# A fused attention and token mixer: the paired last tokens get their attention rows by copies and one add, and the written-out order is new behind the first up projection

## The chip, the core and the metric

The kernel runs on one core of one Trainium2 chip. The metric is the device time of one execution in microseconds. The core has a matrix engine (TensorE, PE in the profile, with its weight loads as PEld), a vector engine (VectorE, DVE), a scalar engine (ScalarE, ACT), a general engine (GpSimd, POOL) and an engine that only issues transfers here (SyncE, SP). Each engine executes its own instructions in the order in which the program gives them; engines wait for one another on semaphores. Matmul results go to eight banks of 512 floats per partition, and VectorE or ScalarE must move them out (evict them) before a bank can be filled again.

## What is computed

Eight batches, eight heads, 576 tokens, head dimension 64. Attention is causal in blocks of 64 tokens; its output is laid out as x of 576 tokens by 512 channels per batch and goes through a mixer: one two-layer network over the tokens, one over the channels, each with a residual.

```python
scores = scale * np.matmul(q, k.transpose(0, 1, 3, 2))
scores = np.where(block_i >= block_j, scores, -1e9)      # blocks of 64
attn = softmax(scores);  x = attn @ v                    # then (B, 576, 512)
h  = np.maximum(x.T @ w_tok1, 0.0) @ w_tok2              # 576 -> 256 -> 576
u  = x + h.T
h2 = np.maximum(u @ w_ch1, 0.0) @ w_ch2                  # 512 -> 1536 -> 512
out = u + h2
```

## The kernel before

**An order written out by hand.** Every step of the kernel is registered with `Plan.add` as an operation with a number, the engines that may run it, its dependencies and a function that issues its instructions. `ORDER` (from L100) is one long string: each word is an operation's number and a letter for its engine (T TensorE, A ScalarE, D VectorE, P GpSimd, S SyncE), followed, for an operation that opens a bank, by the letter of the bank (a to d are the tiles `mm`, e to h the tiles `late`). `Plan.placed` walks through the words and issues the operations, so the string sets the order on every engine, the engine of each eviction and the bank of each product. The planner's costs and priorities in `P.add` play no part in it any more.

**Tiles and stages.** A batch's 576 tokens are four chunks of 128 and a last one of 64. For each batch, `load_qk` loads K and Q for four heads at a time (GpSimd issues the transfer, L418) and VectorE transposes them in 32x32 blocks (L442). `load_v` loads V in pieces J = 0 to 4, one for each chunk (L468, pieces J = 0 to 3 of 128 KB and J = 4 of 64 KB). `score_set` (L566) makes the scores of two or four heads, ScalarE takes their exponential into `e_sb` (L772), `tail` copies the last 64 columns aside (L594) and clears them (L599). `head_out` multiplies the exponentials with V for the four chunks of a head (L616; VectorE's reciprocal L636 and multiply L642 write x into `x_sb`), and `ends_out` does the last 64 tokens (L669, L691, L697).

**The last tokens.** `ends_out` writes chunk 4 of `x_sb` with the heads interleaved: even heads lie on partitions 0 to 63, odd heads on partitions 64 to 127, in 256 columns. A 64-row chunk would leave half of every later product empty, so `token_mix` pairs the last 64 tokens of two batches, b-1 and b for odd b, into one tile `um_sb[:, pair]` of 128 rows by 512 channels. The four pairs together are treated as a ninth batch, the mixed one, at the end.

**The mixer.** `token_up` makes the token hidden layer `aT`. `token_mix` multiplies it with w_tok2 into a bank for each chunk (L902), and VectorE adds x to it on its way into `u_sb` (L917). For a pair it does eight matmuls of the w_tok2 columns 512 to 576 (L933) into the two halves of one bank, and then four matmuls with the identity (L942), which add the attention rows to the bank and put even and odd heads in their columns. An eviction by ScalarE (L400) or VectorE (L402) casts the bank into `um_sb`. u is then transposed, by TensorE for batch 1 and its pair (L989) and by transfers for later ones (L979). The channel layers are `channel_up` for batch 0, `channel_up_half` for batches 1 to 3 and the mixed one and `channel_up_fast` for pairs of later batches; `channel_down_fast` (L1364) makes the last product and folds partial sums and the residual into `o_sb` (L1410). These use fewer products by sums and differences of weights and inputs that VectorE makes first (L1061, L1075, L1316, L1346).

**Around the change.** The order before and the order after hold the same words up to 306P, a tail copy on GpSimd at 31.9 us; from there they differ. Numbers that the prediction names: 264 to 268 are V pieces J = 0 to 4 of batch 1; 427 and 430 are the loads of K and Q for the second four heads of batch 2, and 428 one of VectorE's transposes of that K; 167 to 169 are the first three pieces of w_ch2 (wc2, 512 KB each, L511); 445 is a score set of batch 2 and 624 one of batch 3; 492 is VectorE's multiply that ends a head of batch 2 and, in the new order, frees a bank that 624 takes; 1546 and 1547 are output transfers of the mixed batch, 1558 and 1559 a product and a fold of the last batch, 1590 the last output. TensorE is then in the channel up products of batch 0. `EVAC` marks evictions that VectorE or ScalarE may do, `TAILS` small copies that VectorE or GpSimd may do:

```python
EVAC = ("DVE", "ACT")
TAILS = ("DVE", "POOL")
```

## Time and profile before

| what | value |
| --- | --- |
| time, median of 3 runs (lowest to highest) | 284.84 us (284.7 to 284.98) |
| span of the profiled execution | 283.1 us |
| granted TensorE clock | 0.999 |
| TensorE busy | 276.5 us, 98% of the span |
| VectorE busy, instructions | 239.1 us, 84%, 515 |
| ScalarE busy, instructions | 179.3 us, 63%, 331 |
| GpSimd busy, instructions | 72.4 us, 26%, 126 |
| HBM read, written | 35.85 MB, 9.44 MB |

The span is what the profiler saw from the first to the last instruction; the time of a run holds some 1.8 us around it. A row of a timeline gives the start in us, the length in us, the engine, the line in the kernel, the operation, output and inputs, and in square brackets how long the engine stood idle before it and what ended that. PE rows in which many matmuls are put together give the length of the whole group. "issue" means a wait that the profile shows no cause for. A row for a load ends with the kilobytes of one transfer and the median time in us from issue to landing. In a table of windows each engine has its busy time and the number of its instructions.

### The profile page before, as it was taken

What the parts mean: (1) busy time and instruction counts of PE and PEld (TensorE: products, weight loads), DVE (VectorE), ACT (ScalarE), POOL (GpSimd) and SP (SyncE); (2) the same over time, 40 slices, a digit from 0 to 9 for tenths busy, and PEclk for the clock granted to TensorE, in tenths of its full rate; (3) what the DMA queues carried; (4) which work ended last, traced back from release to release, by engine and by line L of the source; (5) the groups of instructions that cost most, each with busy time, mean ns of one, the idle gap of its engine ahead of it and who ended that gap; (6) DMA issues with size and microseconds to landing.
All of it is one profiled execution on the core that took longest, in us unless ns stands there. A gap on an engine that the chain in (4) does not pass through costs nothing.

```text
span 283.1 us, 9609 instructions
## 1 busy us (share of the span) xinstructions
PE 276.5 (98%) x4110; PEld 204.7 (72%) x4110; DVE 239.1 (84%) x515; ACT 179.3 (63%) x331; POOL 72.4 (26%) x126
## 2 busy tenths in 40 slices
PE   8999999999999999999999999999999999999995
PEld 3566656588776788986877658756789876568884
DVE  4578669999889898999998979959897897579984
ACT  3798788953998856897779866274533744652200
POOL 8885760511631351063232221000000000000000
PEclk9999999999999999999999999999999999999999
DMA  7999999955989792999698595100044502100157
GB/s 174 161 181 198 198 195 200 140 89 113 109 97 135 81 153 55 165 194 166 72 117 144 43 195 67 59 21 19 0 78 91 206 0 76 74 2 2 74 151 223
DMA packets 64891, 31.97 MB, mean 113 GB/s; under 512 B 53200, under 2 KB 55888, under 8 KB 64848
## 3 DMA queue, kind: packets, MB, share of 16 engines
q0 software_dynamic: 44896, 17.49, 53.8%
q1 hardware_dynamic: 19520, 13.21, 19.7%
q8 instruction: 32, 0.52, 0.8%
q10 hardware_dynamic: 432, 0.66, 0.7%
q14 instruction: 11, 0.09, 0.1%
HBM read 35.85 MB, written 9.44 MB: 160 GB/s over the span
## 4 chain that ended last, share of the span: by engine, by line
PE 90%; POOL 3%; ACT 3%; DMA 2%; issue 1%; DVE 0%; POOLq 0%
PE late L1364 23%; PE mm L1103 8%; PE mm L1230 7%; PE mm L566 7%; PE mm L1364 7%; PE late L1230 6%; PE late L1103 6%; PE mm L616 5%; PE mm L807 3%; PE mm L902 2%; PE late L616 2%; PE late L902 2%; PE late L566 2%; DMA vals<-in_v_dram 2%; PE late L1030 2%; PE mm L1030 2%
## 5 line engine op out<-in xcount | busy, mean ns | idle before, releaser
L772 ACT ACTIVATE e_sb<-mm 128x512 bf16<-128x512 f32 x82 | 46.5, 606 | 13.2 <-PE late L566 9.5
L772 ACT ACTIVATE e_sb<-late 128x512 bf16<-128x512 f32 x86 | 48.4, 609 | 9.2 <-PE late L566 8.4
L442 DVE STREAM_TRANSPOSE qk_sb<-qk_sb 128x288 int32<-128x288 int32 (+1 forms) x65 | 41.7, 693 | 3.8 <-PE late L566 1.8
L468 POOL DMA_DIRECT2D vals<-in_v_dram x45 | 36.9, 832 | 4.7 <-PE mm L616 2.4
L1364 PEld LDWEIGHTS <-gT 128*128 128x128 bf16 x336 | 32.0, 98 | 5.6 <-issue 0.4
L1364 PEld LDWEIGHTS <-sums 128*128 128x128 bf16 x324 | 31.3, 98 | 5.2 <-issue 0.4
L566 PEld LDWEIGHTS <-qk_sb 32*64 32x64 bf16 x1280 | 19.6, 104 | 13.1 <-issue 9.2
L566 PE MATMUL mm<-qk_sb 32*64 32x512 bf16 (+7 forms) x560 | 27.4, 289 | 0.1
L566 PE MATMUL late<-qk_sb 32*64 32x512 bf16 (+7 forms) x560 | 26.8, 295 | 0.6 <-ACT e_sb L585 0.3
L616 PEld LDWEIGHTS <-e_sb 128*128 128x128 bf16 x640 | 23.2, 97 | 5.4 <-issue 2.3
L1364 PE MATMUL late<-wd_sb,gT 128*128 128x256 bf16 x168 | 20.7, 273 | 0.0
L1364 PE MATMUL late<-wd_sb,sums 128*128 128x256 bf16 x168 | 20.6, 273 | 0.0
L1103 PEld LDWEIGHTS <-ws_sb 128*128 128x128 bf16 x192 | 18.2, 98 | 3.0 <-issue 0.9
L616 PE MATMUL mm<-vals,e_sb 128*128 128x65 bf16 x450 | 19.9, 193 | 0.1
L642 DVE TENSOR_TENSOR x_sb<-mm,rinv 128x256 bf16<-128x256 f32 x45 | 18.7, 421 | 1.3
L1410 DVE TENSOR_TENSOR o_sb<-late,u_sb 128x512 f32<-128x512 f32 x22 | 14.9, 683 | 3.6 <-PE late L1364 3.6
L1230 PEld LDWEIGHTS <-ws_sb 128*128 128x128 bf16 x120 | 11.6, 98 | 8.6 <-issue 0.2
L1103 PEld LDWEIGHTS <-wc_sb 128*128 128x128 bf16 x144 | 15.3, 114 | 1.4 <-issue 0.4
L1364 PE MATMUL late<-wc_sb,gT 128*128 128x256 bf16 x132 | 16.2, 272 | 0.0
L594 POOL COPY vals<-e_sb 128x256 bf16<-128x256 bf16 (+1 forms) x11 | 4.3, 392 | 40.6 <-ACT e_sb L772 40.4
L400 ACT COPY mm<-late 128x512 f32<-128x512 f32 (+1 forms) x16 | 9.1, 571 | 8.1 <-PE late L1230 5.3
L793 ACT ACTIVATE gT<-mm 128x512 bf16<-128x512 f32 x21 | 12.6, 616 | 1.9 <-PE mm L1103 0.9
(198 smaller groups left out, 631.8 us busy)
## 6 DMA issues: line engine op xcount, KB each, us to landing
out_dram<-o_sb SPq DMA_DIRECT2D x19, 256.0 KB, 2.4
qk_sb<-in_k_dram POOLq DMA_DIRECT2D x14, 288.0 KB, 6.2
qk_sb<-in_q_dram POOLq DMA_DIRECT2D x14, 288.0 KB, 5.9
vals<-in_v_dram POOLq DMA_DIRECT2D x28, 128.0 KB, 4.8
out_dram<-o_sb SPq DMA_DIRECT2D x7, 512.0 KB, 3.5
wc_sb<-in_moe_w_ch_dram POOLq DMA_DIRECT2D x8, 192.0 KB, 7.0
wc_sb<-in_moe_w_ch_dram POOLq DMA_DIRECT2D x3, 512.0 KB, 10.5
vals<-in_v_dram POOLq DMA_DIRECT2D x15, 64.0 KB, 5.4
```

The lines of the kernel that those rows point to most:

```text
L442: nc.vector.transpose(dst[:, 0:S, :] .rearrange("p s e -> p (s e)") .bitcast(I32) .rearrange("p (a k) -> p k a", k=NB)[:, k0:k1], raw2.bit ...
L468: nc.gpsimd.dma_start(out=t[128 - p : 128, J, hs, 0:64], in_=src)
L566: nc.tensor.matmul(out=home(n)[64 * half : 64 * half + 64, c : c + w], lhsT=bar[r, 0] if j is None else kT[i][r, 64 * j : 64 * j + 64, par ...
L616: nc.tensor.matmul(out=u[:, I, 0:65], lhsT=e[:, h, c : c + 128], rhs=vt[:, J, head, 0:65], start=(J == 0), stop=(J == I),)
L642: nc.vector.tensor_tensor(out=xt[:, 0:4, 64 * head : 64 * head + 64], in0=u[:, :, 0:64], in1=ri[:, 0:4].to_broadcast([128, 4, 64]), op=MULT,)
L772: nc.scalar.activation(dst, bank_of(x), EXP, scale=scale)
L793: nc.scalar.activation(dst, src, RELU)
L902: nc.tensor.matmul(out=bank_of(bank), lhsT=w2_sb[:, t, 128 * si : 128 * si + 128], rhs=at[:, t, :], start=(t == 0), stop=(t == NDT - 1),)
L1103: nc.tensor.matmul(out=bank_of(bank)[:, 256 * o_ : 256 * o_ + 256], lhsT=x(o_, m), rhs=y[:, :, m, :], start=opens, stop=m == 1, skip_group ...
L1230: nc.tensor.matmul(out=bank_of(bank)[:, 128 * c : 128 * (c + step)], lhsT=x(m), rhs=y[:, c : c + step, m, :], start=opens, stop=m == 1, sk ...
L1364: nc.tensor.matmul(out=bank_of(bank)[:, 256 * i : 256 * i + 256], lhsT=x[:, kk, 128 * i : 128 * i + 128], rhs=y[:, kk], start=first and i ...
L1410: nc.vector.tensor_tensor(out=dst, in0=src, in1=other, op=ADD)
```

## The change

In `token_mix` each batch gets two copies of its last tokens' attention rows, one for even and one for odd heads (n = 0, 1), from `x_sb` chunk 4 into the batch's 64 rows of `um_sb`, on VectorE or GpSimd. The identity matmuls L942 are gone, the matmuls L933 of the pair end the bank, and VectorE adds the bank to `um_sb` in place, where an eviction on either engine cast it before. The copies take operation numbers from 2000 (two for each batch), so that the others keep theirs; for this `ops` becomes a dictionary.

```diff
     def add(
         self, engines, cost, emit, deps=(), prio=0.0, take=(), give=(), xfer=None, mode=0, at=0.0,
-        urgent=0, until=1e9, quick=False, stick=False,
+        urgent=0, until=1e9, quick=False, stick=False, later=False,
     ):
...
-        o.n = len(self.ops)
-        self.ops.append(o)
+        if later:
+            o.n, self.later = self.later, self.later + 1
+        else:
+            o.n, self.count = self.count, self.count + 1
+        self.ops[o.n] = o
...
         um_rows = []
+        for n in range(2):
+            def emit(o, n=n):
+                dst = umt[64 * odd : 64 * odd + 64].rearrange("p (g n d) -> p g n d", n=2, d=64)[:, :, n]
+                src = xt[64 * n : 64 * n + 64, 4, 0:256].rearrange("p (g d) -> p g d", d=64)
+                (nc.vector if o.engine == "DVE" else nc.gpsimd).tensor_copy(dst, src)
+
+            ends = [op for i, op in enumerate(x_done) if i % (5 if b else 3) == (4 if b else 2)]
+            op = P.add(TAILS, {"DVE": 0.15, "POOL": 0.4}, emit, ends, prio, later=True)
+            xm_done.setdefault(pair, []).append(op)
+            reads(("x", b % 3), op)
...
-                            stop=False,
+                            stop=(t == NDT - 1),
...
-                for n in range(2):
-                    for i in range(2):
-                        nc.tensor.matmul(
-                            out=bank_of(bank)[64 * i : 64 * i + 64, :].rearrange(
-                                "p (g n d) -> p g n d", n=2, d=64
-                            )[:, :, n],
-                            lhsT=ident[:, 64 * n : 64 * n + 64],
-                            rhs=x_sb[(b - 1 + i) % 3][:, 4, 0:256].rearrange("p (g d) -> p g d", d=64),
-                            start=False,
-                            stop=(n == 1),
-                        )
...
             def emit(o, bank=bank):
-                cast(o, umt, bank_of(bank))
-
-            um_rows.append(P.add(EVAC, evac_cost(512), emit, [op], prio, give=[bank]))
+                nc.vector.tensor_tensor(out=umt, in0=bank_of(bank), in1=umt, op=ADD)
+
+            um_rows.append(P.add("DVE", dve_cost(512), emit, [op] + xm_done[pair], prio, give=[bank]))
```

`ORDER` is replaced behind 306P. It holds the same TensorE operations (511 words with T in both), and 549 words for VectorE instead of 515, 314 for ScalarE instead of 333, 124 for GpSimd instead of 121, 36 for SyncE instead of 38. Of the sixteen copies ten go to VectorE (2003 to 2007, 2009, 2011, 2012, 2014, 2015) and six to GpSimd. The first words behind 306P, before and after:

```diff
-    306P 387Tg 353A 267P 426D 384Td 315A 388T 266P 316A 404Ta 385T 317A
-    268P 408Tb 314A 381Te 386D 405A 416Tf 427P 409D 390Tc 389A 307P 391T 333D 430P 372Td 392A 308Tabhg 167P 373T
-    311A 334D 382T 168P 310A 369Tc 309A 370T 169P 417A 375Tb 335D 434P 312A 378Ta 379T 383A 433P 366Th 374A 367T
+    306P 316A 353D 375Tg 315A 266P 427P 378Td 379T 333D 387Ta 416Tb 366Tf 334D 390Te 317A 388T 426D 391T 376T 314A 384Tc
+    417D 389D 385T 377D 392A 307D 308Tgeab 168P 386A 428D 268P 422D 380A 372Th 367T 267P 309A 312A 404Td 430P 405D 423D
+    408Tc 400Tg 429D 373T 369Tb 310A 368A 409A 381Te 370T 382T 311A 295Tc 169P 383A 335D 286Ta 324Tf 401D 296D 289Te
...
-    1581D 1553D 1558Th 1561D 1545D 1564T 1579D 1548S 1549A 1559D 1584T 1565D 1582T 1577D 1585D 1566T 1589A 1583D
-    1556T 1588A 1567D 1562T 1569S 1557D 1586T 1563D 1568S 1587D 1590S
+    1555D 1537D 1550D 1570D 1476D 1540T 1542T 1571D 1541D 1556T 1551D 1478S 1578Ta 1552D 1575A 1560T 1580T 1543D 1546A
+    1558Tf 1572D 1544T 1553D 1547A 1581D 1559D 1579D 1561D 1573D 1562T 1545D 1564T 1563D 1565D 1576T 1584T 1549S 1548S
+    1566T 1557D 1582T 1577D 1585D 1567D 1583D 1586T 1587D 1568A 1588S 1589A 1569A 1590S
```

## The prediction

> **What bounds the kernel now.** I read the page's busy shares and chain first, then TensorE's waits, then the stretch of the timeline behind the point where the two written-out orders part.

> ```profile
> span 283.1 us, 9609 instructions
> PE 276.5 (98%) x4110; PEld 204.7 (72%) x4110; DVE 239.1 (84%) x515; ACT 179.3 (63%) x331; POOL 72.4 (26%) x126
> ```
> ```profile
> DVE  4578669999889898999998979959897897579984
> ```
> ```profile
> PE 90%; POOL 3%; ACT 3%; DMA 2%; issue 1%; DVE 0%; POOLq 0%
> ```

> TensorE is the bound, and VectorE is next, at nine tenths of nearly every slice from 42 us to 135 us. The two longest of TensorE's waits are these:

> ```profile
> PE mm L371 <- DVE wd_sb L344: 1.2, 1, 1.2
> PE sc L566 <- DVE qk_sb L442: 0.6, 1, 0.6
> ```

> Both lie in the opening, before the orders part behind the tail copy 306P at about 32 us. So what the change removes from TensorE is a gain in full, and what the new order lets come late is a loss in full: the old order holds almost no slack to spend. The one stall that I found behind the parting is in front of score set 445 (the issue row of the timeline):

> ```profile
> 52.73 0.11 PEld L566 LDWEIGHTS <-bar 32*64 32x64 bf16 x4 [0.38 <-issue]
> ```

> The sum is made on the profiled span, 283.1 us; the median of the runs, 284.84, lies 1.8 above it, and I carry that over unchanged.

> **Step 1, the identity matmuls.** Four pairs lose four matmuls of 256 columns each. In the chain, in order of time, they stand alone on the path:

> ```profile
> 53.35 0.55 PE mm L933 x4
> 53.90 0.22 PE mm L942 x4
> ```

> The gain is 4 x 0.22 = 0.88 us. The two orders otherwise hold the same TensorE operations, as often in another tile shape than the one in front, so the shuffling itself costs TensorE nothing. The stall of 0.38 belongs to the old sequence; I let it go too: -0.4.

> **Step 2, VectorE's add for the cast, and the copies.** Rows of the tile um_sb and of the tail copies, min/median/max in ns:

> ```profile
> L400 ACT CAST um_sb<-late x2: 586/602/617, 162.4 to 194.6; 128x512 bf16<-128x512 f32 x2
> L402 DVE CAST um_sb<-mm x1: 682/682/682, 122.2 to 122.2; 128x512 bf16<-128x512 f32 x1
> L594 POOL COPY vals<-e_sb x11: 291/402/403, 16.0 to 171.0; 128x256 bf16<-128x256 bf16 x10, 128x128 bf16<-128x128 bf16 x1
> L594 DVE COPY vals<-e_sb x7: 195/226/299, 9.3 to 138.2; 128x256 bf16<-128x256 bf16 x4, 128x128 bf16<-128x128 bf16 x3
> ```

> The add is as long as the cast, but always on VectorE: three evictions leave ScalarE for the engine that has no room. Of the sixteen copies (64 rows by 256) GpSimd gets 6, up to 6 x 0.40 = 2.4 us, and VectorE 10, up to 10 x 0.23 = 2.3 us. The copies hang on attention rows finished long before, so none is itself waited for; GpSimd's price is in its queue, step 3. With seeds, finals and weight sums dealt anew, some 24 evictions move from ScalarE to VectorE in all: 515 VectorE instructions become 549.

> **Step 3, the loads behind 306P.** Old order on GpSimd: V pieces 267 266 268 of batch 1, K of batch 2 (427), Q (430), then wc2 pieces 167 168 169. New: 266, K 427, wc2 piece 168, and only then 268 and 267. The queue in the trace, and the time from issue to landing of the last V piece, of K, and of the wc2 pieces (min/median/max):

> ```profile
> 32.22 2.44 POOL L468 DMA_DIRECT2D vals<-in_v_dram  x3
> 34.63 0.58 POOL L418 DMA_DIRECT2D qk_sb<-in_k_dram  x1
> ```
> ```profile
> 36.04 0.54 POOL L511 DMA_DIRECT2D wc_sb<-in_moe_w_ch_dram  x1
> 36.77 0.53 POOL L511 DMA_DIRECT2D wc_sb<-in_moe_w_ch_dram  x1 [0.20 <-issue]
> ```
> ```profile
> vals<-in_v_dram POOLq DMA_DIRECT2D x1, 64.0 KB, 5.5
> qk_sb<-in_k_dram POOLq DMA_DIRECT2D x1, 288.0 KB, 6.3
> DMA to landing us min/median/max: 8.7/10.5/12.1
> ```

> Issued by 34.0, V is complete at 39.5. K lands at 34.6 + 6.3 = 40.9, the wc2 pieces at 36.0 + 8.7 = 44.7 and 36.8 + 10.5 = 47.3: transfers land in the order of issue, a K after 1.4 us and a wc2 piece after about 2.5. With both ahead of the last V piece it lands at 39.5 + 1.4 + 2.5 = 43.4. TensorE wants it here:

> ```profile
> 41.50 0.77 PE L616 MATMUL mm<-vals,e_sb 128*128 128x65 bf16 x20
> ```

> In both orders the work in front of this is the same length, so it stands 43.4 - 41.5 = 1.9 us. The old cover was 2.0 us and is used up. What is late next: K lands 1.4 after the first V piece instead of after the third, near 39.6, and its transpose, written well ahead in VectorE's new order (behind it stand clips and u work), holds VectorE from about 38.0; TensorE is waiting for V by then, so this lies under the same wait.

> [...]

> **Step 4, VectorE behind the wait.** How the engine fills the old stretches, and the pace of its instructions from start to start (reciprocal and multiply, K transposes, weight sums, adds):

> ```profile
> 31.50:41.50 10.00, 10.00 (x101) 5.45 (x101) 6.46 (x9) 9.21 (x19) 8.19 (x13) 1.00 1.62 192
> 41.50:67.50 26.00, 25.90 (x507) 18.91 (x507) 24.43 (x59) 18.93 (x38) 5.25 (x11) 1.00 0.94 131
> 67.50:72.70 5.20, 5.20 (x130) 4.88 (x130) 4.40 (x13) 3.61 (x8) 2.08 (x6) 1.00 0.94 184
> ```
> ```profile
> 42.29 0.42 DVE L642 TENSOR_TENSOR x_sb<-mm,rinv 128x256 bf16<-128x256 f32 x1
> 42.63 0.17 DVE L636 RECIPROCAL rinv<-mm 128x4 f32<-128x4 f32 x1
> 42.84 0.42 DVE L642 TENSOR_TENSOR x_sb<-mm,rinv 128x256 bf16<-128x256 f32 x1
> ```
> ```profile
> 45.35 0.71 DVE L442 STREAM_TRANSPOSE qk_sb<-qk_sb 128x288 int32<-128x288 int32 x1
> 45.90 0.16 DVE L636 RECIPROCAL rinv<-mm 128x4 f32<-128x4 f32 x1
> ```
> ```profile
> 50.76 1.82 DVE L1316 TENSOR_TENSOR wd_sb<-wc_sb 128x1536 bf16<-128x1536 bf16 x2
> 52.50 1.94 DVE L1316 TENSOR_TENSOR wd_sb<-wc_sb,wd_sb 128x1536 bf16<-128x1536 bf16 x2
> ```
> ```profile
> 55.30 0.68 DVE L917 TENSOR_TENSOR u_sb<-late,x_sb 128x512 bf16<-128x512 f32 x1
> 55.90 0.68 DVE L917 TENSOR_TENSOR u_sb<-mm,x_sb 128x512 bf16<-128x512 f32 x1
> ```

> In the old order VectorE does 59 + 13 = 72 instructions, 28.8 us, in these 31.2. In the new order, from the first head of batch 1 to the multiply 492D, for which score set 624 of batch 3 waits at 72.7 by TensorE's own pace, there are 77: 16 reciprocals of 0.21 and 16 multiplies of 0.34 (8.8), 4 small pairs (1.6), 8 transposes of 0.55 (4.4), 9 weight sums of 0.87 (7.8), 13 adds, folds and evictions of 0.60 (7.8), 7 small ones (1.9): 32.3 us. That exceeds 31.2 by 1.1 before anything is late. It starts no earlier than 43.9 (V at 43.4, then the first products), so 492D ends near 76.2: up to 3.5 us behind, of which 1.9 is the wait for V. The same sum over the old stretch runs slightly high, so I take 3.1 for V and backlog together. Ends: 1.9 (free banks absorb all of VectorE's lag), and 4.5 (V 1 us later, or each of 77 hand-overs a little dearer).

> [...]

> **Step 5, the rest of the order.** Behind 73 us VectorE again has stretches near 100%. An eviction has to fit its bank's turn: I count 47 hand-overs from TensorE through an eviction and back with under 0.25 us to spare, where the old order has 7. Nothing in the trace prices them: 0 if each just fits, 2 if each of 47 costs 0.04; I take 0.5, nearer the first, as the old tight ones show no wait above 0.4.

> **Step 6, the tail.** The last fold 1559D must wait for outputs 1546 and 1547, both issued by ScalarE; TensorE has nine units of six matmuls meanwhile, 0.66 apart:

> ```profile
> 276.15 0.82 PE L1364 MATMUL mm<-wc_sb,sums 128*128 128x256 bf16 x6
> 276.80 0.82 PE L1364 MATMUL late<-wd_sb,vals 128*128 128x256 bf16 x6
> ```
> ```profile
> out_dram<-o_sb SPq DMA_DIRECT2D x19, 256.0 KB, 2.4
> out_dram<-o_sb SPq DMA_DIRECT2D x7, 512.0 KB, 3.5
> ```

> That is 5.9 us of cover for a fold (0.68), two issues, a landing of 2.4 to 3.5 and another fold: 5.0 to 6.5. So 0 to 0.6; I take 0.1.

> **Sum.** -0.88 - 0.4 + 3.1 + 0.5 + 0.1 = +2.4: span 285.5, time 287.2.

> **Rivals.** (a) Only the wait for V bites, and VectorE's surplus hides in free banks: -0.88 - 0.4 + 1.9 + 0.4 = +1.0, 285.8. For it: the old order, too, ran VectorE at 94% here and lost 0.4. (b) The V pieces, 64 and 128 KB, run beside the 512 KB piece and land by 41.5; then VectorE's surplus and K's transpose alone remain, 1.7 to 2.0 less what banks absorb: about +0.8, 285.6. Against it: the landings above. (c) The other side: V is there by 42.2 and VectorE's 77 instructions take under 30.9 us, so nothing is late: -0.88 - 0.4 + 0.2 = -1.1, 283.7. It decides from where all new stalls together stay under 1.3 us; the queue would have to beat its own spacing by 1.2 us. (d) The tight hand-overs cost 2 us or more on top of the forecast: 289 to 290.

> **How the numbers follow.** Forecast 0.57, (a) 0.19, (b) 0.10, (c) 0.07, (d) 0.07. The forecast's own range is 286 to 288.6, by 1.9 to 4.5 for its main term. From 285.0 to 289.8 leaves out (c), a sliver of (b) and of (d). A change under 0.2%, 0.57 us, can hardly be told from none by these runs; so faster means under 284.3: (c), 0.07; same takes the low ends of (a) and (b), 0.07; slower 0.86.

> **What would show it.** No row of an identity matmul into the paired bank; a first head of batch 1 that waits about 1.9 us for the vals load near 41.5; VectorE without a gap from there on; score sets near 70 to 76 waiting for VectorE's multiplies; the rest shifted by about 2 to 3 us, ending with a short wait or none. I am wrong if V lands before 42.2, if VectorE shows gaps in the fifties, or if waits behind 76 us add up to more than 2 us.

## The result and the profile after

The changed kernel took 294.53 us, median of 6 runs (292.94 to 295.34), beside 285.05 us for the kernel before (284.7 to 286.05): a ratio of 1.0311, 95% interval 1.0274 to 1.0348. It is slower by 9.5 us, four times what was predicted and outside the range. The profiled execution has a span of 293.3 us, 10.2 more than before's. (The kernel before took between 284 and 290 us on other chips, mostly with the granted clock, so kernels are compared by their ratio to it on the same chip, and runs with a disturbed clock are left out of the ratios.)

The page of the changed kernel, from its first part, its clock row and its chain:

```profile
span 293.3 us, 9589 instructions
...
PE 278.3 (95%) x4094; PEld 205.1 (70%) x4094; DVE 253.2 (86%) x549; ACT 171.2 (58%) x310; POOL 74.3 (25%) x129
...
PEclk9999889999999999999999999999999999999998
...
PE 82%; DMA 7%; DVE 5%; issue 2%; POOL 1%; ACT 1%; SPq 0%; DVEq 0%
```

TensorE was 98% busy and is 95% busy; 82% of the chain is TensorE's where it was 90%; and the two slices from 29 to 44 us have a clock below 0.9 (as has the last slice, where TensorE has ended). TensorE's waits (waiter, releaser, us in total, times, longest):

```profile
PE late L1029 <- DMA wc_sb<-in_moe_w_ch_dram: 2.4, 2, 1.5
PE mm L568 <- issue: 1.8, 1, 1.8
PE sc L568 <- DVE qk_sb L444: 1.4, 1, 1.4
PE mm L373 <- DVE wd_sb L346: 1.2, 1, 1.2
PE mm L904 <- DVE um_sb L960: 0.6, 1, 0.6
PE late L618 <- issue: 0.5, 1, 0.5
PE late L568 <- ACT e_sb L587: 0.3, 1, 0.3
PE mm L618 <- DMA vals<-in_v_dram: 0.2, 1, 0.2
```

The last row, 0.2 for V, is not the wait that the prediction had at 1.9 us: it stands at 15.35 us, in the opening, before the orders part. At the first head of batch 1, at 45.48, TensorE does not wait for V at all. The first row is new and was in no step: products of the channel up layer (L1029) wait for w_ch1. TensorE's timeline at these places, and the clock in stretches of 2 us (the number behind POOL's is the granted clock):

```profile
15.35 0.40 PE L618 MATMUL mm<-vals,e_sb 128*128 128x65 bf16 x8 [0.24 <-DMA vals<-in_v_dram]
...
32.77 0.38 PE L1029 MATMUL late<-uT,wc_sb 128*128 128x512 bf16 x1 [0.89 <-DMA wc_sb<-in_moe_w_ch_dram]
34.62 0.41 PE L1029 MATMUL late<-uT,wc_sb 128*128 128x512 bf16 x1 [1.47 <-DMA wc_sb<-in_moe_w_ch_dram]
34.87 2.69 PE L1029 MATMUL mm<-uT,wc_sb 128*128 128x512 bf16 x6
...
45.48 0.77 PE L618 MATMUL mm<-vals,e_sb 128*128 128x65 bf16 x20
```
```profile
34.00:36.00 2.00, 1.38 (x4) 0.56 (x5) 1.36 (x2) 0.01 (x1) 1.53 (x2) 0.74 2.16 160
36.00:38.00 2.00, 2.00 (x9) 1.03 (x8) 1.18 (x2) 0.00 (x0) 1.38 (x3) 0.50 1.72 199
38.00:40.00 2.00, 2.00 (x9) 0.94 (x8) 1.13 (x2) 0.01 (x1) 1.49 (x3) 0.91 1.10 219
```

Right behind 306P the new order runs product 375, of columns 6, which needs all eight pieces of w_ch1; the last two land at 33.7 and 34.6. The old order ran columns 10 and 9 there, which need only the second half; in before the first of them started at 32.1 without a wait. Behind the wait the granted clock fell to half: (1 - 0.74) + (1 - 0.50) + (1 - 0.91), times 2 us, is 1.7 us. So the first head of batch 1 starts at 45.5, not 41.5.

The chain of the changed kernel has another gap that no semaphore explains, inside score set 1082:

```profile
153.37 0.00 PE mm L568
153.37 1.81 issue
155.19 0.38 PE mm L568
```

And the end. First TensorE's last product and then, from the list of transfers, the last output (KB, us from issue to landing), of after and then of before:

```profile
286.67 0.82 PE L1363 MATMUL late<-wd_sb,vals 128*128 128x256 bf16 x6
```
```profile
out_dram<-o_sb SPq DMA_DIRECT2D x1, 128.0 KB, 3.9
```
```profile
278.77 0.82 PE L1364 MATMUL mm<-wd_sb,vals 128*128 128x256 bf16 x6
```
```profile
out_dram<-o_sb SPq DMA_DIRECT2D x1, 128.0 KB, 1.9
```

TensorE ends at 287.5 and the span 5.8 us later; before, at 279.6 and 3.5 us later.

To place the rest I set each product's start against the one in front of it and took off the usual distance of such a pair (its median in before's trace). That gives TensorE's own work 0.93 shorter, and what it lost where:

| part of the 10.2 us | us |
| --- | --- |
| TensorE's own work (identity matmuls) | -0.9 |
| waits for w_ch1 | +2.3 |
| slow clock behind them | +1.7 |
| wait for a V piece of batch 2, at 65 us | +0.2 |
| the two stalls without a semaphore (score set 1082, head 664) | +2.9 |
| hand-overs with VectorE and ScalarE, less the old order's stalls (the largest for um_sb at 59 us, 0.7) | +1.7 |
| from TensorE's end to the end of the span | +2.3 |

### The profile page after: what moved, and what is told of

Read it like the earlier page. It is cut to its first block, busy times and chain, and to the rows that moved or that the text cites. A ratio compares the mean times of both kernels' runs of the same rounds, so it can differ in the third digit from the quotient of the medians.

```text
span 293.3 us, 9589 instructions
## 1 busy us (share of the span) xinstructions
PE 278.3 (95%) x4094; PEld 205.1 (70%) x4094; DVE 253.2 (86%) x549; ACT 171.2 (58%) x310; POOL 74.3 (25%) x129
## 4 chain that ended last, share of the span: by engine, by line
PE 82%; DMA 7%; DVE 5%; issue 2%; POOL 1%; ACT 1%; SPq 0%; DVEq 0%
PE late L1363 19%; PE mm L1363 9%; PE late L1102 7%; PE mm L1229 6%; PE late L1229 6%; PE mm L1102 6%; DMA wc_sb<-in_moe_w_ch_dram 5%; PE mm L568 4%; PE mm L618 3%; PE late L568 3%; PE late L618 3%; PE mm L904 2%; PE late L904 2%; PE mm L809 2%; PE late L809 2%
## 5 line engine op out<-in xcount | busy, mean ns | idle before, releaser
L1363 PEld LDWEIGHTS <-gT 128*128 128x128 bf16 x336 | 32.1, 98 | 5.6
L568 PE MATMUL mm<-qk_sb 32*64 32x64 bf16 (+7 forms) x550 | 27.2, 290 | 1.9 <-issue 1.8
L568 PE MATMUL late<-qk_sb 32*64 32x64 bf16 (+7 forms) x570 | 26.4, 293 | 0.3 <-ACT e_sb L587 0.3
L1363 PE MATMUL late<-wd_sb,sums 128*128 128x256 bf16 x138 | 17.0, 273 | 0.0
L618 PE MATMUL mm<-vals,e_sb 128*128 128x65 bf16 x380 | 16.6, 193 | 0.3 <-DMA vals<-in_v_dram 0.2
L402 ACT COPY mm<-late 128x512 f32<-128x512 f32 (+1 forms) x14 | 7.8, 564 | 15.4 <-PE late L1363 8.9
L795 ACT ACTIVATE gT<-mm 128x512 bf16<-128x512 f32 x16 | 9.5, 600 | 11.8 <-PE mm L1102 6.5
L644 DVE TENSOR_TENSOR x_sb<-mm,rinv 128x256 bf16<-128x256 f32 x38 | 15.7, 416 | 0.6
L420 POOL DMA_DIRECT2D qk_sb<-in_q_dram x14 | 7.9, 561 | 30.8 <-DVE x_sb L644 17.5
L795 ACT ACTIVATE gT<-late 128x512 bf16<-128x512 f32 x16 | 9.6, 608 | 9.0 <-PE late L1029 6.4
L1363 PE MATMUL late<-wd_sb,gT 128*128 128x256 bf16 x120 | 14.7, 273 | 0.0
## 6 DMA issues: line engine op xcount, KB each, us to landing
out_dram<-o_sb SPq DMA_DIRECT2D x17, 256.0 KB, 2.3
qk_sb<-in_k_dram POOLq DMA_DIRECT2D x14, 288.0 KB, 5.6
qk_sb<-in_q_dram POOLq DMA_DIRECT2D x14, 288.0 KB, 5.0
out_dram<-o_sb SPq DMA_DIRECT2D x7, 512.0 KB, 2.8
wc_sb<-in_moe_w_ch_dram POOLq DMA_DIRECT2D x3, 512.0 KB, 10.4
out_dram<-o_sb ACTq DMA_DIRECT2D x4, 256.0 KB, 3.9
```

The source lines that it names most:

```text
L568: nc.tensor.matmul(out=home(n)[64 * half : 64 * half + 64, c : c + w], lhsT=bar[r, 0] if j is None else kT[i][r, 64 * j : 64 * j + 64, par ...
L618: nc.tensor.matmul(out=u[:, I, 0:65], lhsT=e[:, h, c : c + 128], rhs=vt[:, J, head, 0:65], start=(J == 0), stop=(J == I),)
L644: nc.vector.tensor_tensor(out=xt[:, 0:4, 64 * head : 64 * head + 64], in0=u[:, :, 0:64], in1=ri[:, 0:4].to_broadcast([128, 4, 64]), op=MULT,)
L795: nc.scalar.activation(dst, src, RELU)
L1363: nc.tensor.matmul(out=bank_of(bank)[:, 256 * i : 256 * i + 256], lhsT=x[:, kk, 128 * i : 128 * i + 128], rhs=y[:, kk], start=first and i ...
```

## Experiments

**Is it the order or the pairs' change?** e1 has the new `token_mix` with before's order, e2 the old one with after's order.

```diff
 # e1: ORDER of before; 2000 to 2015 all on GpSimd, behind the multiplies they need
-515A ... 1115A ... 1361A
+515D ... 1115D ... 1361D
 # e2: ORDER of after without its words 2000 to 2015, token_mix of before
```

> The new token_mix with the order of before: identity matmuls gone, all sixteen copies on GpSimd behind the multiplies that they need, the four adds on VectorE where the casts stood. Theory (the order is what costs, the change of the pairs is worth its 0.88 us): 285.05 - 0.88, and up to 0.4 back for three more evictions on VectorE: 284.2 to 284.6, and no wait for um_sb over 0.3 us. Rival (the copies and adds are what costs, because VectorE or GpSimd is late with them): 286 or more, with TensorE waiting for um_sb or for the loads behind the copies.

> The old token_mix (identity matmuls, no copies) with the order of after, the four casts on VectorE. Theory: all of the loss is the order's, so 294.5 + 0.9 = 295.4, between 294.3 and 296.5, with the same wait for the last w_ch1 piece near 33 us and the same slow clock behind it. Rival (the copies cost): under 290.

e1: 287.19 us, ratio 1.0038 (0.9991 to 1.0084). e2: 295.49, ratio 1.0291 (1.0213 to 1.0368), as much as after, with the same wait for w_ch1 (2.5 us). So the loss comes with the order (the stalls without a semaphore, which vary from execution to execution, are a part of it in both; see e14 below). But e1 missed its expectation: the 0.88 did not show as a gain. By the reckoning of distances its trace has 3.05 us of stalls where before's has 0.94, most of them where `token_mix` and the products behind it take over banks.

**What took e1's gain?** e12 is before with the three casts on VectorE alone, no copies, identity matmuls kept.

```diff
-515A ... 1115A ... 1361A
+515D ... 1115D ... 1361D
```

> Before with one thing of the pairs' change: the casts of pairs 0, 2 and 3 on VectorE instead of ScalarE (pair 1's is there already); identity matmuls stay, no copies. The run with the whole change in before's order had 3.05 us of stalls of TensorE behind 32 us where before has 0.94. Theory (moving these evictions to the engine without room is what cost there): stalls of 2 to 3 us near 54 to 60, 129, 165 and 198 us, time 1 to 2 over before. Rival (the copies on GpSimd cost, by their port or their place in the queue): stalls as before, under 1.3 us in all, same time as before.

286.56 us, ratio 1.0045 (1.0025 to 1.0066), 1.3 us over before, and 1.6 us of stalls in the trace instead of 0.94. The time went as the theory had it, the stalls were smaller than it had them. Moving three evictions to VectorE costs 1.3 us (0.7 to 1.9 by the interval), at least about as much as the sixteen identity matmuls (0.9). What the copies cost on GpSimd is not told apart: e1 lies where the cast's price less the matmuls' gain would put it, within its interval.

**The wait for w_ch1.** e3 runs the products of columns 9 to 11 first; e4 keeps the order and fills the wait with matmuls whose results are overwritten.

```diff
 # e3
-306P 316A 353D 375Tg 315A 266P 427P 378Td 379T 333D 387Ta 416Tb 366Tf 334D 390Te 317A 388T
+306P 316A 353D 387Ta 315A 266P 427P 390Te 333D 416Tb 366Tf 334D 388T 317A 426D 391T
+314A 384Tc 417D 389D 385T 392A 375Tg 376T 378Td 377D 379T 307D
 # e4, in channel_up, cc = 6, first half
+for _ in range(11):
+    nc.tensor.matmul(out=bank_of(bank), lhsT=ident, rhs=w2_sb[:, 0, 0:512], start=True, stop=True)
```

> After, but behind 306P the products of columns 10, 11 and 9 of the channel up layer, which need only the second half of w_ch1, run before those of columns 6 and 7, which need all eight pieces. Theory: no wait for w_ch1 (2.3 us less) and no slow clock from it (1.7 less); TensorE then comes to the first head of batch 1 at 41.5 and waits for V, which landed at 43.7 in after: 2.2 back. 294.5 - 4.0 + 2.2 = 292.7; up to 294.4 if this second wait slows the clock as the first did. Rival (V is in time whenever it is asked for): 290.5. Rival (w_ch1 is not what TensorE waits for): no change, 294.5.

> After with eleven identity matmuls of 512 columns, 0.21 us each, into the bank of the first product behind 306P, in front of that product: TensorE works through most of the wait for w_ch1. The extra results are overwritten. Theory (the idle wait lets the granted clock fall to half, and this costs 1.7 us on top of the wait): clock 1.0 throughout, matmuls of 512 columns at 379 ns near 36 us instead of 634, time 294.5 - 1.7 = 292.8. Rival (the matmuls are slow there for another reason, such as the transfers of that time): still 634 ns, 294.5.

e3: 292.06, ratio 1.0189 (1.0108 to 1.0271). By the ratios this is 3.5 us under after (1.0311) and 2.1 under the second measurement of after (1.0264, e5 below), where 1.8 was expected. It still waits 0.9 us for w_ch1, since product 366, which I had left in front, needs a late piece too, and 0.7 for V at the first head of batch 1. It has a new wait as well, 0.8 us near 32 us for a VectorE eviction into uT; e7 to e10, e13 and e14, which also run columns 9 to 11 first, have the same one. e4: 293.94, ratio 1.0243 (1.0159 to 1.0326), an interval that holds after's ratio too, so e4 is read by its trace alone. TensorE and the clock in it:

```profile
31.55 2.55 PE L1029 MATMUL late<-w_sb,ident 128*128 128x512 bf16 x11
33.93 0.38 PE L1031 MATMUL late<-uT,wc_sb 128*128 128x512 bf16 x1
34.62 0.41 PE L1031 MATMUL late<-uT,wc_sb 128*128 128x512 bf16 x1 [0.31 <-DMA wc_sb<-in_moe_w_ch_dram]
34.86 1.46 PE L1031 MATMUL mm<-uT,wc_sb 128*128 128x512 bf16 x6
...
43.80 0.77 PE L618 MATMUL mm<-vals,e_sb 128*128 128x65 bf16 x20
```
```profile
36.00:38.00 2.00, 2.00 (x14) 1.16 (x13) 1.82 (x4) 0.00 (x0) 1.41 (x3) 1.00 1.71 199
```

The same six matmuls behind the wait take 1.46 us instead of 2.69 and the first head comes at 43.8 instead of 45.5: 1.7 us, with the wait for the data as long as before. So the transfers do not slow these matmuls; the granted clock does. That idle time brought the slow clock is likely, but e4 alone does not show it, since the clock also stayed at 1.00 in e2's trace, which has the wait in full (2.5 us) and nothing to fill it. Over all traces, of four with 2.2 to 2.5 us of idle time in a wait between 31 and 41 us three have the fall (after, e6, e7; not e2), and none of those with 1.5 to 1.8 has it (e3, e5, e8). Idle time is not the only thing in front of a fall, either: in e9's trace the clock is 0.50 from 18.6 to 28.8 us, behind some 1 us of idle time in the 3.5 us before.

The falls in after, e6 and e7 last 3.41 us each, and half of that is the 1.7 us lost. In front of after's stood 2.4 us of idle time within 2.75.

**After again, with the outputs early, with the opening mended, with both.**

```diff
 # e6: product 1544 and its fold 1545 ahead of the last batch's folds; 1549 issued by ScalarE
-1560T 1580T 1543D 1546A 1558Tf 1572D 1544T 1553D 1547A 1581D 1559D 1579D 1561D 1573D 1562T 1545D 1564T ... 1549S 1548S
+1560T 1543D 1544T 1546A 1580T 1558Tf 1572D 1553D 1545D 1547A 1549A 1548S 1561D 1581D 1559D 1579D 1564T 1562T 1573D ...
 # e7: columns 9 to 11 first, 366 behind 379, GpSimd 266 267 268 427 168, transposes 428 and 429 behind 293 and 291; e8: e6 and e7
```

> After itself, beside the next three on the same chip and for a second trace. Theory: the wait for the last w_ch1 piece at 33 to 34.6 us, the wait for um_sb at 59 us and the late outputs stand at the same places and sizes (2.3, 0.7 and 2.0 us); the stalls inside score sets and heads that no semaphore explains (2.2 us at 153 us, 0.55 at 95) move or change in size, since they come from TensorE's instruction fetch getting its turn among the loads. Rival: these stand at the same places and sizes too, and belong to the order. Time 293 to 296.

> After, with the tail alone mended: product 1544 and its fold 1545 run before the last batch's folds 1559 and 1579, so that the outputs 1548 and 1549 leave some 2 us earlier against the end of TensorE's work, and 1549 is issued by ScalarE instead of behind 1548 on SyncE. Theory (after's span ends 5.8 us behind TensorE's last product, before's 3.5, because 1.6 MB of output starts 1.3 us later and is bound by the transfer rate): 2.0 less than after, and the last product to the end of the span 3.8 us. Rival (the end of the span is set by the last output alone): no change, 5.8 us.

> After with its first 12 us mended: products of columns 9 to 11 first, so that nothing waits for w_ch1; the V pieces 266 268 267 ahead of K, and the transposes 428 and 429 of that K behind the first heads. Theory (4.0 us lie in the wait for w_ch1 and the clock behind it; V comes in time once its pieces go first): the first head of batch 1 at 42 instead of 45.5, 3.5 to 4.0 less than after, unless VectorE's backlog takes some of it back: TensorE's wait for um_sb near 56 us then grows from 0.7 to 1.5. Rival (VectorE's work, 77 instructions of 32 us, sets the pace to 73 us whatever stands in front): all but 1 us is lost again by 75 us.

> After with both mended, the first 12 us and the outputs. Theory: the two add up, 5.5 to 6 less than after, and 3 to 4 us over before are left, in VectorE's lateness and in instruction fetches. Rival (the late stages are bound by something else that takes the gain back): 3 us less than after or less.

| run | us | ratio (interval) | TensorE's end to the end of the span |
| --- | --- | --- | --- |
| e5 | 293.43 | 1.0264 (1.0201 to 1.0327) | 5.8 |
| e6 | 292.55 | 1.0211 (1.0134 to 1.0288) | 3.8 |
| e7 | 293.46 | 1.0265 (1.0201 to 1.0328) | 5.8 |
| e8 | 289.94 | 1.0156 (1.009 to 1.0222) | 3.7 |

e5 is the kernel of after, and its ratio shows how far two measurements of one kernel can lie apart, 1.0264 and 1.0311. The outputs were right by the last column, 2.0 to 2.1 us in the traces of both pairs; the times of e5 and e6 alone do not tell the two apart. In e6 the last product ends at 288.0 and the span at 291.8 (timeline, then the last output in the list of transfers):

```profile
287.21 0.82 PE L1366 MATMUL late<-wd_sb,vals 128*128 128x256 bf16 x6
```
```profile
out_dram<-o_sb SPq DMA_DIRECT2D x1, 128.0 KB, 1.8
```

The last output lands 1.8 us after its issue again instead of 3.9. That e6 also gives 1549 to ScalarE is not told apart from the earlier issue. My reading is that the last output was queued behind the mixed batch's, which after issues only here (times of SyncE's issues in after, first the mixed batch's):

```profile
284.31 1.37 SPq L1438 DMA_DIRECT2D out_dram<-o_sb  x2
287.33 1.12 SPq L1454 DMA_DIRECT2D out_dram<-o_sb  x2
```

In the later kernels with the same end the last column is 3.7 (e14) to 4.5 us (e10).

e7 missed: my mend made a new wait. VectorE's weight sums 333 and 334, which need all of w_ch1, stood ahead of the evictions 377, 389 and 417, and score set 308 waited 2.2 us for them, in e7 with a slow clock behind it again. e8 with the same fault lost 1.7 us there and no clock. So e8 missed too: by the ratios it is 3.1 us under e5, where 5.5 to 6 was expected.

**V, with the fault mended.** e9 and e13 (one kernel) have the sums behind the evictions, the outputs early and after's load order; e10 the same with V first; e11 is before with V late.

```diff
 # e9, e13, e10
+... 384Tc 417D 389D 307D 385T 392A 375Tg 376T 378Td 377D 333D 334D 426D 379T 366Tf 308Tgeab
 # e10 besides: 266P 267P 268P 427P ... 168P; 428D and 429D behind 293D and 291D
 # e11, order of before: 306P ... 266P ... 427P ... 167P ... 268P ... 267P ... 307P 430P ... 168P
```

> After with the outputs early as before and the first 5 us mended without the fault of the last two runs (there VectorE's weight sums 333 and 334 stood ahead of the evictions 417, 389 and 377 and waited for w_ch1 themselves; now they stand behind). GpSimd's loads are after's: K and a w_ch2 piece ahead of V. Theory (the prediction's step on V was right, and only hidden behind the wait for w_ch1): TensorE comes to the first head of batch 1 near 42 and waits there for V, which lands near 43.7, about 1.7 us; 288.5 to 290. Rival (something else is late at this place anyway): no wait for V over 0.5 us.

> The same with V ahead of K and w_ch2, and K's transposes behind the first heads. Theory: no wait for V, 1.7 us less than the run beside it, unless VectorE's backlog takes its place; the prediction's running sum (77 instructions, 32.3 us, for 31.2) then leaves TensorE about 1 us of waits for VectorE up to 73 us. Rival (VectorE sets the pace up to 73 us): the 1.7 us come back as such waits and the times of the two are the same.

> Before with one thing of after: behind 306P GpSimd issues 266, K 427, a w_ch2 piece, then 268 and 267. Theory: the last V piece lands at 43.4 instead of 39.5, TensorE waits 1.9 us at 41.5, and nothing of it is won back: 1.9 over before, 3.5 if the wait lets the clock fall. Rival (V pieces are in time or the wait is absorbed): 0.5 over before or less.

> The kernel of e9 again, for a trace of an undisturbed run. Theory (prediction's step on V): TensorE comes to the first head of batch 1 at 42 to 42.5, waits 1.3 to 1.7 us for V, and then has less left to wait for VectorE than e10 had (2.5 us up to 67 us). Rival (VectorE's work sets the pace up to 73 us, V or no V): up to 67 us the stalls come to 2.5 us in both, and the times of the two kernels are the same within 0.3 us.

e11: 288.86 us, ratio 1.0104 (1.0073 to 1.0134), 3.6 over before. Its trace has the wait that the prediction described, near the end of the first head:

```profile
41.74 0.43 PE L616 MATMUL mm<-vals,e_sb 128*128 128x65 bf16 x9
43.23 0.49 PE L616 MATMUL mm<-vals,e_sb 128*128 128x65 bf16 x11 [1.06 <-DMA vals<-in_v_dram]
```

A head is ten matmuls, and the piece that lands last here is 267, J = 3, which only the tenth reads. Nine of the first head's ten run, and the tenth waits, so 1.2 us are lost by the usual distance and not 1.9. Three of the nine runs, the profiled one among them, were 1.2 to 1.7 over before, at a mean clock of 1.00; the other six, five of them with 0.98 to 0.994, 2.8 to 4.2. So the wait itself is 1.2 in the one trace, and the rest goes mostly with the clock; whether it fell behind this wait is not shown, as no trace of such a run was kept.

On the new order V is worth less. e9: ratio 1.0174 (1.013 to 1.0217); e13, the same kernel on another chip: 1.0223 (1.0176 to 1.0271); e10: 1.0164 (1.0133 to 1.0195). e13's TensorE loses 1.7 us at the heads to V and VectorE; up to 67 us e10's stalls are 2.5 us over before's, nearly all of it for VectorE: 0.8 for the eviction into uT at 33.5 and the rest in these rows:

```profile
46.16 0.59 PE L1032 MATMUL late<-uT,wc_sb 128*128 128x512 bf16 x2 [0.26 <-DVE x_sb L647]
47.04 0.46 PE L621 MATMUL late<-vals,e_sb 128*128 128x65 bf16 x10 [0.29 <-DVE x_sb L647]
...
53.19 0.30 PE L571 MATMUL mm<-qk_sb 32*64 32x320 bf16 x1 [0.23 <-DVE gT L800]
58.55 0.59 PE L907 MATMUL mm<-aT,w_sb 128*128 128x512 bf16 x2 [0.82 <-DVE um_sb L963]
```

So VectorE's surplus is real, and it takes back most of what an earlier V would bring. How much exactly the times do not settle: e9 and e10, on one chip, differ by 0.3 us, and e13 and e10, on two chips, by 1.7, with intervals that overlap in both pairs. The traces say 0.6: from TensorE's weight load 570 to 1600, which is from 32.1 to 93.2 us in e10, e10 takes 61.1 us, e14 (below, the same order) 61.1 and e13 61.7. None of the mended orders comes within 4 us of before, and what is left of the loss in them I have not placed in full.

**The stalls without a semaphore.** e14 is e10 with 63 more matmuls in the opening, the same columns in all.

```diff
 # raise_clock, n < 21
-nc.tensor.matmul(out=bank_of(bank)[:, 0:256], lhsT=zeros[:, 0:128], rhs=zeros[:, 0:256], ...)
+for c in range(0, 256, 64):
+    nc.tensor.matmul(out=bank_of(bank)[:, c : c + 64], lhsT=zeros[:, 0:128], rhs=zeros[:, c : c + 64], ...)
```

> The kernel of e10 with 21 of the opening's filler matmuls of 256 columns cut into four of 64, the same columns in all: 63 more matmuls and weight loads, so that every later instruction of TensorE stands 126 places further on, about half of a 16 KB fetch. Theory (the stalls are late fetches): no stall at the tenth matmul of head 664 (0.54 in e10) or at the end of score set 1082 (0.45); if fetches 12, 13 and 20 are late again, the stall stands 126 instructions earlier in the stream, near 92 and 148.5 us. Rival (they belong to what these operations do): both stalls at the same operations as before. Time within 1 us of e10's.

291.85 us, ratio 1.025 (1.0215 to 1.0285): 1.8 us more than e10 (2.5 by the ratios), so the expectation of 1 us was missed. The trace has the difference before the orders part: the same weight load (570 in e10) starts 1.9 us later, and the stalls without a semaphore in front of it come to 2.6 us (0.40, 0.76 and 1.45) where e10's come to 1.0. The stalls at head 664 (in e10 the row at 94.65) and score set 1082 are gone; one of 1.04 stands in a product of the channel down layer (e14's row):

```profile
94.65 0.39 PE L621 MATMUL late<-vals,e_sb 128*128 128x65 bf16 x7 [0.35 <-issue]
```
```profile
100.24 0.61 PE L1368 MATMUL mm<-wc_sb,gT 128*128 128x256 bf16 x4 [1.04 <-issue]
```

Counting weight loads from the start shows what they share. In nine traces (after, e2, e4, e6 to e10, e13) such stalls stand behind 863, 1630 to 1632, 1758 to 1760 or 2654 to 2656 weight loads, that is at distances of 6, 1 and 7 times 128: on a grid of 256 instructions of TensorE, a weight load and a matmul being two. In e14, with everything 63 pairs further on, the stall stands behind 1760 again, at another operation; those of its opening stand behind 224, 480 and 608, on the same grid. All 36 idle times of TensorE over 0.15 us that end in "issue" in the sixteen traces lie on it. Before has two of them as well, in its opening, behind 352 and 480 weight loads:

```profile
22.13 0.38 PE L566 MATMUL late<-qk_sb 32*64 32x512 bf16 x1 [0.26 <-issue]
28.05 0.38 PE L855 MATMUL mm<-w_sb,aT 128*128 128x512 bf16 x1 [0.33 <-issue]
```

In the list of transfers a fetch of 16 KB of instructions precedes each: in after, for the stall that ends at 155.19 (2.2 us lost by the usual distances), this one (a window of 0.3 us at 152.7; packets and MB), which lasts until 153.8:

```profile
q8 instruction: 1, 0.02, 20.3%
```

The stalls end 1.2 to 1.6 us behind their fetch. In all 496 blocks of the sixteen traces (from weight load 224 on, every 128th) the first weight load starts 1.2 us or more behind the end of the block's fetch, also where nothing stalls. So they are instruction fetches that come too late, and belong to no operation. Behind the point where the orders part they come to between next to nothing and 3.2 us an execution (e3 and e6). They are no fixed part of the new order: in e5, the kernel of after again, TensorE is idle under 0.15 us where it was idle 0.55 and 1.81 in after. Before's trace has none there. What holds a fetch back is not shown: loads were in flight in front of the late ones, but also in front of others that were in time, and taking loads away there was not tried.

## Why the prediction was wrong

The direction was right, the size and the main step were not. Two steps failed: step 3, which took the work in front of the first head to be free of new waits (they and the clock came to 4.0 us), and step 6, which put the tail at 0.1 us (it was 2.3). Besides, 2.9 us of late instruction fetches were in no step. Step by step:

- **Step 1, the identity matmuls.** Right: TensorE's own work is 0.93 shorter. The old stall in front of 445 did not return in after either.
- **Step 2, the copies.** The prices were right: 0.22 us on VectorE, 0.40 on GpSimd (median 222 and 398 ns). That no copy is waited for was right too. "Three evictions leave ScalarE for the engine that has no room" was a remark and not a term of the sum; e12 measured 1.3 us for it in before's order. In after eight of the ten copies on VectorE neither overlap with the instruction in front nor with the one behind (two of the eight write rows 0 to 63 but read rows from 64 up), and the two that read and write rows 0 to 63 overlap by 0.08. Timeline of VectorE in after, first a copy that does not overlap, then one that does:

```profile
115.63 0.22 DVE L930 COPY um_sb<-x_sb 64x256 bf16<-64x256 bf16 x1
115.88 0.69 DVE L1409 TENSOR_TENSOR o_sb<-late,u_sb 128x512 f32<-128x512 f32 x1
116.49 0.22 DVE L596 COPY vals<-e_sb 128x256 bf16<-128x256 bf16 x1
116.62 0.21 DVE L930 COPY um_sb<-x_sb 64x256 bf16<-64x256 bf16 x1
116.76 0.41 DVE L644 TENSOR_TENSOR x_sb<-late,rinv 128x256 bf16<-128x256 f32 x1
```

- **Step 3, V.** The landing was right: 34.86 + 8.8 = 43.7 for the last piece, 43.4 predicted. Wrong was the sentence "in both orders the work in front of this is the same length, so it stands 43.4 - 41.5 = 1.9 us". The work has the same length, but its first product waits for w_ch1: I had checked the new order against the landings of V and K and not against those of w_ch1, which had no wait in the old one. With 4.0 us lost in front, the first head came at 45.5, 1.8 us behind the landing, and V cost nothing there. In before's order, where nothing is in front, it cost 1.2 (e11): the step was right as a mechanism and 0.7 too dear, since it let the whole head wait for a piece that only the tenth matmul reads.
- **Step 4, VectorE.** VectorE is busy without a gap, as predicted (27.0 of 27.5 us from 45.5 us on in after), and its surplus shows as TensorE's waits of about 1 us up to 73 us in after and some 1.6 in e10, where V is on time. The place was wrong: no score set near 70 to 76 us waits for VectorE in either trace; the waits stand earlier, the largest for um_sb (0.6 and 0.8). The 3.1 us for "V and backlog together" were in fact 4.0 for w_ch1 and clock, none for that V and some 1 for VectorE.
- **Step 5, hand-overs.** 0.5 predicted, with 0 to 2; behind 73 us about 1 us is lost so. What the step did not hold are the fetches, 2.9 us in this execution.
- **Step 6, the tail.** Wrong by 2.2. I priced the wait of fold 1559D for two outputs (it is there, 0.7 us of VectorE's, and costs TensorE nothing) and not what the later issue of 1548 and 1549 does to the outputs behind them.
- **The rivals.** (d) had the size in mind, 289 to 290, but only for hand-overs; the measured time lies beyond all cases. What the two missing terms of the order, w_ch1 and the outputs, have in common: each stands at a place where the old trace shows no wait, because the old order had kept it clear. The third, the fetches, is not the new order's alone: before has two in its opening.

## What to carry to other kernels

When an order is dealt anew, check every operation that is moved forward against the landing of every transfer that it reads, not only against the transfers that were moved: the one that costs can be one that stayed. An idle TensorE may cost more than the wait, since the clock can fall behind it, as it did behind the longest waits in three of four traces here (to 0.50 for 3.41 us, 1.7 us lost). And see to the outputs before the last products: what is still to be written when TensorE ends is paid in full (5.8 us from there to the end of the span in after, 3.5 in before).
